# The opening stage written as one sequence: norm, transposes and v's first three products of chunk 0

## The chip, the cores and the metric

The kernel runs on one core of one Trainium2 chip. The metric is the device time of one execution in microseconds (us). Engines are named as in the profile: PE (matrix products; PEld its weight loads), DVE (VectorE), ACT (ScalarE), POOL (GpSimd) and SP (SyncE, which here issues every DMA).

## The reference

`x` has 2048 rows of 1024 values. One layer norm feeds a linear attention with 32 heads and a gated GLU; the two results are multiplied and added to `x`.

```
xn = layernorm(x)                                  # 2048 x 1024
q, k, v = split(xn @ wqkv)                         # 32 heads of 32
phi(a)  = [softmax(a @ w_phi), softmax(-(a @ w_phi))]   # per head, 64 features
o  = phi(q) @ (phi(k)^T v) / (phi(q) @ sum(phi(k)) + 1e-6)
s  = o @ wo
g  = silu((sigmoid(xn @ w_gate) * (xn @ w_up)) @ w_down)    # inner size 3584
out = x + s * g
```

## The kernel before, in words

**Products.** Every large matrix product is cut in two along rows of x, along the inner dimension and along columns, and is done as seven block products in place of eight; their operands are raw blocks (`B11`, `B21`, `B22`) or sums of blocks (`T1` to `T4`). The sums are made once for x and once for the weights. To keep fp32 accuracy each operand is split in two parts, high (a cast by ACT) and low (the difference, by DVE); `split` (L122) issues both, and `mm3` (L127) issues three matmuls of 128x512 (L129, L130, L131) for each pair of parts.

**Order of the work.** The 2048 rows are two chunks of 1024 rows (8 tiles of 128 rows). Chunk 0 comes first: the projections v, k and q, each as seven block products in the order `B11, B21, T2, T3, T4, T1, B22` (48 matmuls each, accumulated in PSUM banks 0 to 3), then the GLU's gate and up products, in which the norm of chunk 1 is done in the background (`x_task`). Chunk 1 follows, then `w_down`, attention and the output.

**The opening.** `x_load` fetches the tiles of x. `norm` (L154) takes statistics on DVE (L161, L162), the root on ACT (L167), the inverse on DVE (L168) and seven tiny steps on POOL (L166, L170 to L175; for chunk 1 on DVE), and normalises a tile on ACT (L177). `transpose` (L187) turns a tile by eight PE transposes (L193) into banks 4 to 7, from where `operand` splits `B11` and `B21`, and ACT copies the raw blocks to SBUF (L197). `x_sums` (L201) forms the sums of blocks: T2 and T3 on DVE, T1 and T4 on POOL (L205). `v_sums` (L248) forms the sums of v's weight blocks, four of two halves each: two on DVE, two on POOL (L253).

**Side steps.** The tiles after the first, `v_sums`, the four K folds, `x_rest` and the four Q folds are a queue (`side`), of which one entry is issued after each quarter of a block product. `fold` (L272) multiplies a raw block of wqk with the per-head `w_phi` on PE (L281, 16 matmuls a fold), copies four results to SBUF on ACT (L282), lets POOL form four sums (`w_sums`, L227 to L230) and stores seven operands to DRAM (`wf_d`, L283), from which the K and Q products later load their weights. K's folds use the SBUF of block `x1` as buffers, two sets by turns, and raw blocks in block `x2`. `x_rest` makes the operands of B22 (in `x1`), T1 (in `x2`) and T4 (in `x6`), so it takes `x1` over once every K fold is stored.

**What sets the order on an engine.** The tile framework's scheduler orders the instructions of each engine by program order and its own time model; each engine then runs its list strictly in order, and waits on semaphores for the others. `tc.issue_after(i)` keeps an instruction behind another one.

Of the kernel before, what the change touches and what calls it, by code (L numbers as in the profile page):

```python
# [2 lines left out]

# [45 lines left out]
def hedgehog_glu_kernel(  # L49
# [17 lines left out]

    ident = sb.tile([P, P], F32, name="ident")
    make_identity(nc, ident)

    wf_d = dram.tile([3, 7, P, 4, HB], F32, name="wf_d")
    wo_d = dram.tile([7, 4, P, 2 * HB], F32, name="wo_d")
# [28 lines left out]
    block("fb", 43, 4, F32)  # L101
    block("fc", 47, 8, F32)
    NW = 8
    WARM = 28

    banks = [psum.tile([P, HB], F32, name=f"bank{i}") for i in range(8)]

    def whole(i):
        return slots[i].rearrange("p a n -> p (a n)")

    def halves(*ids):
        return [slots[i][:, a] for i in ids for a in range(2)]

    def run(i, n):

        name, k = where[i]
        return blocks[name][0][:, k:k + n]
# [4 lines left out]
    def split(o, src):  # L122

        nc.scalar.copy(o[0], src)  # L124
        return nc.vector.tensor_sub(o[1], src, o[0].bitcast(F32))  # L125
# [19 lines left out]
    XO = {B11: 16, T2: 12, T3: 0, B21: 20, T1: 8, T4: 24, B22: 4}  # L145
    tps = Ring(banks[4:])

    last_norm, last_chain = [], []
# [5 lines left out]
    def norm(tiles, xs):  # L154
        n = len(tiles)
        st = small.tile([P, 2, 2, 6], F32, name=f"bn{tiles[0]}", tag="bn")
        mv = small.tile([P, 2, 2], F32, name=f"mv{tiles[0]}", tag="mv")
        ws = small.tile([P, 4, 2], F32, name=f"lnw{tiles[0]}", tag="lnw")
        for i, xt in enumerate(xs):
            for a in range(2):  # L160
                nc.vector.bn_stats(st[:, i, a], xt[:, a * HB:(a + 1) * HB])  # L161
            nc.vector.bn_aggr(mv[:, :, i], st[:, i])  # L162
        v, r, a, b = [ws[:, q, :n] for q in range(4)]
# [6 lines left out]
        eng.tensor_mul(a, r, r)  # L170
        eng.tensor_mul(a, a, v)
        eng.tensor_scalar(b, a, -0.5, 1.5, op0=ALU.mult, op1=ALU.add)
        eng.tensor_mul(r, r, b)
        eng.tensor_mul(b, mv[:, 0, :n], r)
        last_chain[:] = [eng.tensor_scalar(b, b, -1.0, None, op0=ALU.mult).ins]  # L175
        for i, xt in enumerate(xs):
            last_norm[:] = [nc.scalar.activation(xt, xt, AF.Identity, bias=b[:, i:i + 1], scale=r[:, i:i + 1]).ins]  # L177

    def operand(c, i, u, b):

        if c == 0:
            o, cs = run(XO[i], 4), slice(u * P, (u + 1) * P)
            split((o[:, :, 0, cs], o[:, :, 1, cs]), b.rearrange("p (k t) -> p k t", t=P))
        else:
            nc.sync.dma_start(xo_d[i, :, u], b)

    def transpose(t, xt, dst):  # L187

        c, th, u = t // CTT, t % CTT // 4, t % 4
        for q in range(2):  # L190
            tp = tps.next()
            for k in range(4):
                nc.tensor.transpose(tp[:, k * P:(k + 1) * P], xt[:, (4 * q + k) * P:(4 * q + k + 1) * P], ident)  # L193
            i = {(0, 0): B11, (1, 0): B21, (1, 1): B22}.get((q, th))
            if c == 0 and th == 0:
                operand(c, i, u, tp)
            nc.scalar.copy(dst[q], tp)  # L197
            if c and i is not None:
                operand(c, i, u, dst[q])

    def x_sums(c, u, first, second):  # L201
        (b11, b21), (b12, b22) = first, second
        t2 = b22 if c else b12
        for i, o, a, b in ((T1, b11, b12, b11), (T3, b12, b22, b12), (T2, t2, b22, b11), (T4, b21, b21, t2)):
            (nc.vector if c == 0 and i in (T2, T3) else nc.gpsimd).tensor_sub(o, a, b)  # L205
            if c or i in (T2, T3):
                operand(c, i, u, o)

    def load_operand(i):
        o = run(XO[i], 4)  # L210
# [33 lines left out]
    def v_load(i):  # L244
        r, f, kh = ((39, 0, 0), (41, 0, 1), (45, 1, 0), (36, 1, 1))[i]
        nc.sync.dma_start(row4(r), v_block(f, kh))

    def v_sums():  # L248
# [257 lines left out]

    def x_task(t):
        xt = x_load(t, 52)
        norm([t], [xt])
        th, u = t % CTT // 4, t % 4  # L510
        transpose(t, xt, halves(53 + th))
        if th:
            x_sums(t // CTT, u, halves(53), halves(54))

# [167 lines left out]

    XS = (24, 25, 26, 27, 52, 53, 24, 25)
    first = [halves(i) for i in (50, 51, 54, 38)]
    b12s, b22s = Ring(halves(10)), halves(8, 9)
    xts = [x_load(0, XS[0])]  # L690
    phraw = whole(47)[:, :KT * DH].rearrange("p (g f) -> p g f", f=DH)
    nc.sync.dma_start(phraw, w_phi.rearrange("(g p) f -> p g f", p=P))
    v_load(0)
    xts += [x_load(t, XS[t]) for t in range(1, 4)]
    v_load(1)
    xts += [x_load(t, XS[t]) for t in range(4, 6)]

    def x_tiles(*tiles):
        norm(tiles, [xts[t] for t in tiles])
        for t in tiles:  # L700
            if t < 4:
                transpose(t, xts[t], first[t])
            else:
                b = b12s.next(), b22s[t - 4]
                transpose(t, xts[t], b)
                x_sums(0, t - 4, first[t - 4], b)
            if t < 2:
                xts.append(x_load(t + 6, XS[t + 6]))
            if t == 1:
                v_load(2)  # L710
                v_load(3)

    def x_rest():
        for i, name, src in ((B22, "x1", b22s), (T1, "x2", [b[0] for b in first]), (T4, "x6", [b[1] for b in first])):
            block(name, XO[i], 4, F32R)
            for u in range(4):
                operand(0, i, u, src[u])
        fraw.items = halves(43, 54)


    for n in range(WARM):
        nc.tensor.transpose(banks[3][:, n % 4 * P:(n % 4 + 1) * P], ident, ident)
    with tc.high_priority():
        x_tiles(0)
    with tc.issue_after(last_norm[0]):
        while prep():
            pass
    one = whole(44)[:, :P]
    nc.gpsimd.memset(one, 1.0)
    nc.scalar.copy(ones, one)  # L730
    nc.gpsimd.memset(bd, 0.0)

    def phi_blocks():
        with tc.issue_after(last_chain[0]):
            for j in range(4):
                nc.gpsimd.tensor_copy(bd[j * DH:(j + 1) * DH, :, j * DH:(j + 1) * DH], phraw[j * DH:(j + 1) * DH])

    def todo(f, *a):
        side.append(lambda: f(*a))
# [12 lines left out]
    pmm = Ring(banks[:4])  # L752
    gmm = Ring(banks[:4])
    pbank, gbank = {}, {}
    ur = Ring(halves(50, 51))
# [22 lines left out]
                tasks.popleft()()  # L778

    for n, (kind, c, what, i) in enumerate(ops):  # L780
        ws = ready[n]
        if kind == "proj":
            for u in range(4):
                if i in opening:
# [274 lines left out]
```

## Time and profile before

| what | value |
|---|---|
| executions timed, us | 2425.05, 2435.57, 2437.88 (median 2435.57) |
| profiled execution, us | 2428.84, of which the span of instructions is 2427.1 |
| mean granted PE clock | 0.995 |
| PE busy over the span | 2387.5 us (98%) |
| DVE, ACT, POOL busy | 71%, 42%, 41% |
| DMA | 599.44 MB, mean 247 GB/s |

A window line of the profile gives, for a stretch of the span, the busy time of each engine with its number of instructions, the granted PE clock (1.00 is full speed) and the DMA share. A timeline line gives the start, the duration, the engine, the line of the kernel, the operation, what it writes and reads, the count, and in brackets how long the engine was idle before and what released it. Matmuls are pipelined, so a busy PE isn't PE at full rate.

### The profile page before, as it was taken

Reading aid. Unit: us, or ns where it says so; the run is one execution under the profiler, and the core shown is the slowest. Engines: PE = TensorE matmul, PEld = TensorE weight load, DVE = VectorE, ACT = ScalarE, POOL = GpSimd, SP = SyncE. Lnnn points to the kernel's source line nnn. Section 1 sums busy time; section 2 is a strip of 40 time slices with the busy share of each in tenths; the row PEclk is TensorE's granted clock in tenths of the full one; section 3 lists DMA queues with packets and bytes.
Section 4 is the critical chain, followed back from the end, with each engine's and each line's share of the span. In section 5 each row is a group of like instructions: output and inputs, shape, how many; then the busy total and the mean of one; then the engine's idle time right before and its main releaser. Section 6 shows DMA issues by size and latency. Waiting matters only on the chain. (4 is left out here: it accounts for less than half of the span.)

```text
span 2427.1 us, 32021 instructions
## 1 busy us (share of the span) xinstructions
PE 2387.5 (98%) x11076; PEld 1985.6 (82%) x11076; DVE 1717.7 (71%) x2247; ACT 1007.9 (42%) x1499; POOL 991.4 (41%) x665
## 2 busy tenths in 40 slices
PE   7999999999999999999999999999999999999998
PEld 6887888888888878888888888888888887878887
DVE  6546577777777679747867888646888988855555
ACT  6443244445444344324444444423443334443332
POOL 5542245665666432222344232323333435414554
PEclk8999999999999999999999999999999999999999
DMA  7898767777777787787777666686666666877554
GB/s 276 277 342 317 246 234 258 268 262 256 256 266 257 247 292 252 245 284 238 268 265 261 220 218 221 201 294 241 219 239 227 221 210 224 288 237 243 182 175 150
DMA packets 233234, 599.44 MB, mean 247 GB/s; under 512 B 30576, under 2 KB 30576, under 8 KB 228464
## 3 DMA queue, kind: packets, MB, share of 16 engines
q1 hardware_dynamic: 233072, 597.40, 71.4%
q8 instruction: 87, 1.43, 0.2%
q14 instruction: 75, 0.61, 0.1%
HBM read 361.10 MB, written 236.19 MB: 246 GB/s over the span
## 5 line engine op out<-in xcount | busy, mean ns | idle before, releaser
L129 PE MATMUL bank<-x,w 128*128 128x512 f32 x2352 | 912.3, 390 | 4.5 <-DVE fc L914 1.9
L130 PE MATMUL bank<-x,w 128*128 128x512 f32 x2352 | 915.8, 389 | 0.0
L131 PE MATMUL bank<-x,w 128*128 128x512 f32 x2352 | 907.1, 389 | 0.0
L124 ACT CAST w<-fa 128x512 fp32r<-128x512 f32 (+1 forms) x444 | 308.0, 698 | 543.2 <-PE bank L130 377.6
L129 PEld LDWEIGHTS bank<-x,w 128*128 128x128 f32 x2352 | 441.4, 188 | 97.8 <-DVE fc L914 2.3
L125 DVE TENSOR_TENSOR w<-fa,w 128x512 fp32r<-128x512 f32 (+1 forms) x444 | 432.2, 978 | 122.7 <-ACT w L124 113.9
L131 PEld LDWEIGHTS bank<-x,w 128*128 128x128 f32 x2352 | 441.6, 188 | 91.9 <-DVE w L125 0.4
L130 PEld LDWEIGHTS bank<-x,w 128*128 128x128 f32 x2352 | 441.7, 188 | 90.5 <-DVE x L125 0.2
L129 PE MATMUL bank<-w,x 128*128 128x512 f32 x708 | 278.8, 394 | 4.8 <-DVE fb L391 2.3
L131 PE MATMUL bank<-w,x 128*128 128x512 f32 x708 | 278.0, 393 | 1.6 <-DVE x L125 1.6
L130 PE MATMUL bank<-w,x 128*128 128x512 f32 x708 | 277.7, 392 | 0.0
L850 POOL TENSOR_TENSOR fb<-fb,fc 128x512 f32<-128x512 f32 x57 | 88.5, 1552 | 242.8 <-DVE fc L849 217.8
L129 PEld LDWEIGHTS bank<-w,x 128*128 128x128 f32 x708 | 134.0, 189 | 33.6 <-ACT x L124 3.1
L131 PEld LDWEIGHTS bank<-w,x 128*128 128x128 f32 x708 | 133.8, 189 | 29.6 <-DVE x L125 2.3
L590 POOL TENSOR_TENSOR fc<-fc 128x1024 f32<-128x1024 f32 x32 | 81.8, 2556 | 186.2 <-ACT fc L426 131.1
L130 PEld LDWEIGHTS bank<-w,x 128*128 128x128 f32 x708 | 134.0, 189 | 27.2
L125 DVE TENSOR_TENSOR w<-fb,w 128x512 fp32r<-128x512 f32 (+1 forms) x114 | 106.1, 931 | 39.1 <-ACT w L124 37.6
L849 DVE TENSOR_TENSOR fc<-fc,bank 128x512 f32<-128x512 f32 x84 | 57.3, 682 | 101.4 <-PE bank L131 91.9
L124 ACT CAST w<-fb 128x512 fp32r<-128x512 f32 (+1 forms) x114 | 71.4, 626 | 133.6 <-PE bank L130 97.1
L125 DVE TENSOR_TENSOR x<-fa,x 128x512 fp32r<-128x512 f32 x112 | 113.2, 1011 | 19.3 <-ACT x L124 19.0
L602 POOL TENSOR_TENSOR fc<-fc,sa 128x1024 f32<-128x1024 f32 x32 | 70.2, 2193 | 98.3 <-DVE sa L599 98.3
L124 ACT CAST p<-fc 128x512 fp32r<-128x512 f32 x82 | 64.6, 788 | 107.2 <-DVE fc L442 61.0
(254 smaller groups left out, 3266.4 us busy)
## 6 DMA issues: line engine op xcount, KB each, us to landing
ws_d<-w SPq DMA_DIRECT2D x112, 512.0 KB, 3.8
w<-ws_d SPq DMA_DIRECT2D x112, 512.0 KB, 4.8
fa<-w_gu SPq DMA_DIRECT2D x84, 512.0 KB, 3.9
fa<-h_d SPq DMA_DIRECT2D x84, 512.0 KB, 4.2
fa<-wf_d SPq DMA_DIRECT2D x32, 1024.0 KB, 6.7
h_d<-fc SPq DMA_DIRECT2D x120, 256.0 KB, 3.4
fc<-e_d SPq DMA_DIRECT2D x48, 512.0 KB, 3.6
fc<-qkv_d SPq DMA_DIRECT2D x80, 256.0 KB, 4.5
```

Of the source, the lines that this page charges most:

```text
L124: nc.scalar.copy(o[0], src)
L125: return nc.vector.tensor_sub(o[1], src, o[0].bitcast(F32))
L129: nc.tensor.matmul(o, a[0], b[0], start=first, stop=False, **kw)
L130: nc.tensor.matmul(o, a[0], b[1], start=False, stop=False, **kw)
L131: nc.tensor.matmul(o, a[1], b[0], start=False, stop=last, **kw)
L590: nc.gpsimd.tensor_mul(ez, e, zb)
L602: nc.gpsimd.tensor_mul(e3, e3, r2[:, :, None].to_broadcast([P, 32, DH]))
L849: v = nc.vector.tensor_add(b, u2 if q == 3 else u1, bank)
L850: nc.gpsimd.tensor_mul(g, g, b)
```

## The change

Chunk 0's opening is no longer left to the scheduler. A string `FIRST` lists some 170 steps by short names, and `in_order` gives each instruction of PE, DVE, ACT and POOL a dependency on the one before it on its engine, so that each engine keeps the listed order. The steps cover all eight tiles' norm (`bn`, `sq`, `rc`, `ch`, `n`), the transposes (`T`), the splits of x (`xh`, `xl`) and of the weights (`wh`, `wl`), the raw blocks (`k`), the sums T3 and T2 (`T3s`, `T2s`), two weight sums (`s3`, `s2`), the matmuls of v's products B11, B21 and T2 (`m`) and the reading out of B11's and B21's banks (`e`).

Within that: the norm's tiny steps go from seven on POOL to four fused ones on DVE (`scales`, for chunk 1 too); x's first tile and the first weight block are loaded in halves; `w_phi` and the later weight blocks are loaded after all eight tiles; the raw blocks of tiles 0 to 3 are summed on POOL from the two split parts, where ACT copied them from PSUM; T2 of x is T3 plus B11; the low part of B21's weights is made on POOL; T2's weights need two sums (both on DVE), and two further sums follow on POOL; five more warming transposes stand ahead of the first tile. After `FIRST`, POOL is kept to the order `phi_blocks`, `t4`, `v_sums`, `t1`. All that is left of the side queue (the folds, `x_rest`, the stores of two weight sums) is issued after the last listed instruction of every engine. All of v's B11, B21 and T2 now end before the first fold.

The core of the diff:

```diff
-        eng = nc.gpsimd if tiles[0] < CTT else nc.vector
-        eng.tensor_scalar_add(v, mv[:, 1, :n], EPS_LN)
-        nc.scalar.activation(a, v, AF.Sqrt)
-        nc.vector.reciprocal(r, a)
-        eng.tensor_mul(a, r, r)
...
+        fused = nc.vector.scalar_tensor_tensor
+        def rest():
+            fused(a, v, EPS_LN, r, op0=ALU.add, op1=ALU.mult)
+            fused(a, a, -0.5, r, op0=ALU.mult, op1=ALU.mult)
+            fused(r, a, 1.5, r, op0=ALU.add, op1=ALU.mult)
+            fused(b, mv[:, 0, :n], -1.0, r, op0=ALU.mult, op1=ALU.mult)
...
-    v_first = {B11: 39, B21: 41, T2: 39, T3: 45, T4: 39, T1: 36, B22: 41}
+    v_first = {B11: 39, B21: 41, T2: 36, T3: 45, T4: 45, T1: 39, B22: 41}
...
     def v_sums():
-        vec, pool = nc.vector.tensor_tensor, nc.gpsimd.tensor_tensor
-        for f, o, a, b, op in ((vec, 3, 2, 3, "add"), (vec, 2, 0, 2, "subtract"),
-                               (pool, 0, 3, 0, "subtract"), (pool, 1, 1, 0, "subtract")):
+        for o, a, b, op in ((0, 3, 0, ALU.add), (1, 1, 3, ALU.subtract)):
             for h in range(2):
-                f(whole(VA[o] + h), whole(VA[a] + h), whole(VA[b] + h), op=getattr(ALU, op))
-        for i in (T2, T3, T1, B22):
+                v_sum(nc.gpsimd, o, a, b, op, h)
...
+        elif kind == "k":
+            t, q = int(rest[0]), int(rest[1])
+            if t < 4:
+                hi, lo = [o.bitcast(F32) for o in operand((B11, B21)[q], t)]
+                nc.gpsimd.tensor_add(by_k(first[t][q]), hi, lo)
+            else:
+                nc.scalar.copy((b12s, b22s)[q][t - 4], xbank(t, q))
...
+                nc.vector.tensor_sub(t3s[u], b22s[u], b12s[u])
+                nc.vector.tensor_add(t2s[u], t3s[u], first[u][0])
...
+    with in_order(mybir.EngineType.PE, mybir.EngineType.DVE, mybir.EngineType.Activation, POOL):
+        for name in FIRST:
+            (do_other if name[0] in "mewT" or name.startswith("n0q") else do)(name)
...
+    with after_first():
+        for u in range(4):
+            split(operand(T3, u), by_k(t3s[u]))
+        v_store(T2, T3)
+        while prep():
+            pass
+    with in_order(POOL):
+        phi_blocks()
+        t4()
+        v_sums()
+        t1()
...
-    todo(x_tiles, 1)
-    todo(lambda: (x_tiles(2, 3), phi_blocks()))
-    todo(x_tiles, 4, 5)
-    todo(v_sums)
-    todo(x_tiles, 6, 7)
     for k in range(4):
         todo(fold, K, k)
     todo(x_rest)
+    todo(v_store, T1, B22)
     for k in range(4):
         todo(fold, Q, k)
```

More of the change, by code (lines that the diff above doesn't have):

```diff
@@ L179, in operand @@
[L179 to L199, printed above, removed]
@@ L201, in x_sums, with scales, root, inverse @@
-    def x_sums(c, u, first, second):
-        (b11, b21), (b12, b22) = first, second
[L203 to L207, printed above, removed]
+    def scales(n, mv, ws):
+        v = mv[:, 1, :n]
+        r, a, b = [ws[:, q, :n] for q in range(3)]
+        fused = nc.vector.scalar_tensor_tensor
+        def root():
+            nc.scalar.activation(a, v, AF.Sqrt, bias=eps)
+        def inverse():
+            nc.vector.reciprocal(r, a)
+        def rest():
[3 more added lines that the diff above has]
+            fused(b, mv[:, 0, :n], -1.0, r, op0=ALU.mult, op1=ALU.mult)
+        return root, inverse, rest
@@ new lines, in stats, with norm @@
+    def stats(t, n=1):
+        st = small.tile([P, 2, 2, 6], F32, name=f"bn{t}", tag="bn")
+        mv = small.tile([P, 2, 2], F32, name=f"mv{t}", tag="mv")
+        ws = small.tile([P, 3, 2], F32, name=f"lnw{t}", tag="lnw")
+        return st, mv, ws
+    def norm(t, xt):
+        st, mv, ws = stats(t)
+        for a in range(2):
+            nc.vector.bn_stats(st[:, 0, a], xt[:, a * HB:(a + 1) * HB])
+        nc.vector.bn_aggr(mv[:, :, 0], st[:, 0])
+        for f in scales(1, mv, ws):
+            f()
+        nc.scalar.activation(xt, xt, AF.Identity, bias=ws[:, 2, :1], scale=ws[:, 0, :1])
@@ new lines, in operand, with by_k, transposed, x_sums @@
+    def operand(i, u):
+        o, cs = run(XO[i], 4), slice(u * P, (u + 1) * P)
+        return o[:, :, 0, cs], o[:, :, 1, cs]
+    def by_k(b):
+        return b.rearrange("p (k t) -> p k t", t=P)
+    def transposed(t, q, xt, tp):
+        for k in range(4):
+            nc.tensor.transpose(tp[:, k * P:(k + 1) * P], xt[:, (4 * q + k) * P:(4 * q + k + 1) * P], ident)
+    def x_sums(u, first, second):
+        (b11, b21), (b12, b22) = first, second
+        for i, o, a, b in ((T1, b11, b12, b11), (T3, b12, b22, b12), (T2, b22, b22, b11), (T4, b21, b21, b22)):
+            nc.gpsimd.tensor_sub(o, a, b)
+            nc.sync.dma_start(xo_d[i, :, u], o)
@@ L508, in x_task @@
         xt = x_load(t, 52)
-        norm([t], [xt])
+        norm(t, xt)
         th, u = t % CTT // 4, t % 4
-        transpose(t, xt, halves(53 + th))
+        for q in range(2):
+            tp, b = tps.next(), slots[53 + th][:, q]
+            transposed(t, q, xt, tp)
+            nc.scalar.copy(b, tp)
+            i = {(0, 0): B11, (1, 0): B21, (1, 1): B22}.get((q, th))
+            if i is not None:
+                nc.sync.dma_start(xo_d[i, :, u], b)
         if th:
-            x_sums(t // CTT, u, halves(53), halves(54))
+            x_sums(u, halves(53), halves(54))
     dsteps = [(i, j, (0, 1)) for i in order[:-1] for j in range(NJ)]
@@ L683, in attend @@
         return out
-    XS = (24, 25, 26, 27, 52, 53, 24, 25)
+    XS = (24, 25, 26, 27, 52, 53, 6, 7)
     first = [halves(i) for i in (50, 51, 54, 38)]
-    b12s, b22s = Ring(halves(10)), halves(8, 9)
-    xts = [x_load(0, XS[0])]
-    phraw = whole(47)[:, :KT * DH].rearrange("p (g f) -> p g f", f=DH)
-    nc.sync.dma_start(phraw, w_phi.rearrange("(g p) f -> p g f", p=P))
[L693 to L711, printed above, removed]
+    b12s, b22s = halves(10, 26), halves(8, 9)
+    t3s, t2s = halves(52, 53), halves(27, 24)
+    xts = [whole(i) for i in XS]
+    for a in range(2):
+        nc.sync.dma_start(slots[XS[0]][:, a], x[:P, a * HB:(a + 1) * HB])
+    for h in range(2):
+        nc.sync.dma_start(slots[39 + h], v_block(0, 0)[:, 2 * h:2 * h + 2])
+    for t in range(1, 4):
+        x_load(t, XS[t])
+    v_load(1)
+    for t in range(4, 8):
+        x_load(t, XS[t])
+    v_load(2)
+    v_load(3)
+    phraw = slots[11][:, 1, :KT * DH].rearrange("p (g f) -> p g f", f=DH)
+    nc.sync.dma_start(phraw, w_phi.rearrange("(g p) f -> p g f", p=P))
     def x_rest():
@@ L716, in x_rest @@
             for u in range(4):
-                operand(0, i, u, src[u])
+                split(operand(i, u), by_k(src[u]))
         fraw.items = halves(43, 54)
[L721 to L727, printed above, removed]
     one = whole(44)[:, :P]
@@ new lines, in normalized, with xbank, x_parts, w_parts @@
+    def normalized(t, cs=slice(0, D)):
+        _, _, ws, i, _ = scale[t]
+        nc.scalar.activation(xts[t][:, cs], xts[t][:, cs], AF.Identity, bias=ws[:, 2, i:i + 1], scale=ws[:, 0, i:i + 1])
+    def xbank(t, q):
+        return banks[4 + (2 * t + q) % 4]
+    def x_parts(t, q):
+        if q == "t":
+            return operand(T2, t - 4), by_k(t2s[t - 4])
+        return operand((B11, B21)[q], t), by_k(xbank(t, q))
+    def w_parts(n, h):
+        o = run(28 + (4 * n + 2 * h) % NW, 2)
+        return (o[:, :, 0], o[:, :, 1]), slots[v_first[order[n]] + h]
@@ new lines, in hedgehog_glu_kernel, with in_order @@
+    for n in range(WARM):
+        nc.tensor.transpose(banks[3][:, n % 4 * P:(n % 4 + 1) * P], ident, ident)
+    queued = {}
+    @contextmanager
+    def in_order(*engines):
+        traced = nc.cur_bb.bb.instructions
+        last = traced[-1]
+        yield
+        start = next(k for k in reversed(range(len(traced))) if traced[k] is last) + 1
+        for i in traced[start:]:
+            if i.engine in engines:
+                if i.engine in queued:
+                    tc.add_manual_dep(i, queued[i.engine].name,
+                                      mybir.DependencyInfo(mybir.DependencyClass.NoSync, mybir.DependencyReason.DATA),
+                                      reason="in_order")
+                queued[i.engine] = i
@@ L746, in hedgehog_glu_kernel, with entry @@
+    with in_order(POOL):
[3 more added lines that the diff above has]
+        t1()
+    def todo(f, *a):
+        def entry():
+            with after_first():
+                f(*a)
+        side.append(entry)
     for k in range(4):
@@ L783, in hedgehog_glu_kernel @@
             for u in range(4):
+                if n == 2:
+                    pbank[u] = pmm.next()
+                    step()
+                    continue
                 if i in opening:
```

137 lines of the change are left out of this document (112 added, 25 removed).

## The prediction

> **What bounds the kernel now.** I began with the busy time by stretch, to see where PE, busy 98% of the span, still loses time.
>
> ```profile
> core 0: us, PE busy (x) PEld busy (x) DVE busy (x) ACT busy (x) POOL busy (x), PEclk, DMA share, GB/s
> 0.00:60.00 60.00, 46.10 (x212) 38.79 (x213) 38.08 (x57) 40.56 (x62) 32.20 (x55) 0.83 0.75 276
> 60.00:120.00 60.00, 57.93 (x339) 49.49 (x338) 34.98 (x40) 26.02 (x43) 33.10 (x23) 1.00 0.83 276
> 120.00:200.00 80.00, 77.60 (x368) 64.60 (x367) 39.53 (x42) 29.38 (x43) 32.73 (x23) 1.00 0.94 330
> 200.00:800.00 600.00, 600.00 (x2681) 497.48 (x2680) 424.20 (x574) 263.24 (x387) 320.70 (x220) 1.00 0.74 261
> ```
>
> At full clock a 128x512 matmul follows the last one after 0.2275 us and a 128x128 after 0.0905 us (timeline, 200 us and later). The timeline has 98 and 114 of them before 60 us: 22.3 + 10.3 = 32.6 us of work, so 27.4 us are lost there. From 60 to 200 us it has 470 and 234, 128.1 us of work: 11.9 us lost. From 200 to 800 us nothing is lost. So only the first 200 us, 39.3 us of loss in all, can be won by this change. PE's waits up to 120 us say on what:
>
> ```profile
> engine line waited for: us in total, times, longest us
> PE bank L193 <- ACT x L177: 5.7, 2, 3.3
> PE bank L193 <- ACT x L197: 3.6, 1, 3.6
> PE bank L131 <- DVE x L125: 1.6, 1, 1.6
> ```
>
> They are the norm's chain and the raw copies, which the change attacks; the rest of the loss is half clock (PEclk 0.83). But POOL and DVE hinder each other, and the change moves work between these two, so I looked at their timelines next (DVE, then POOL, then ACT).
>
> ```profile
> 58.92 1.75 DVE L125 TENSOR_TENSOR x<-fc,x 128x512 fp32r<-128x512 f32 x1
> 60.60 1.78 DVE L125 TENSOR_TENSOR x<-x,x 128x512 fp32r<-128x512 f32 x1
> 62.30 0.68 DVE L125 TENSOR_TENSOR x<-fc,x 128x512 fp32r<-128x512 f32 x1
> ```
>
> ```profile
> 68.36 1.74 POOL L227 TENSOR_TENSOR x<-x 128x512 f32<-128x512 f32 x1
> ...
> 96.60 1.29 POOL L230 TENSOR_TENSOR x<-x 128x512 f32<-128x512 f32 x1
> ```
>
> ```profile
> 107.08 2.18 ACT L124 CAST x<-x 128x512 fp32r<-128x512 f32 x4 [6.53 <-DMA qkv_d<-fc]
> 109.16 0.58 ACT L282 COPY fc<-bank 128x512 f32<-128x512 f32 x1
> 110.26 1.66 ACT L124 CAST x<-fc 128x512 fp32r<-128x512 f32 x3 [0.52 <-DVE x L125]
> ```
>
> A DVE step with both inputs in SBUF takes 0.68 us alone and 1.75 beside a POOL sum; that sum takes 1.27 to 1.30 alone and 1.62 to 1.85 beside such steps: they go by turns, about 1.7 us a pair. The four K folds' 16 sums run from 68.36 to 97.89 us. 9.2 us later, their stores landed, ACT splits B22's operand (107.08) over the folds' buffers and, behind it, T1's (110.26); PE begins v's product T1 at 114.3, just as it is done with T4. So this second chain is nearly critical already.
>
> **How I worked it out.** I followed the changed program's lists, engine by engine, giving each instruction its row's duration and starting it when its engine, its semaphores and the DVE/POOL turn allow; loads land 2.35 us and stores 1.4 us after issue, plus 0.66 us for each 256 KB (before's landings). The same on the old lists loses 27.9 us up to 60 (trace 27.4), ends the K sums at 98.2 (97.89) and loses 32.2 up to 200 (39.3, so it misses 7). All "by the lists" below is this.
>
> **The front.** The first tile lands in halves, some 3.8 and 4.4 us (512 KB landed at 4.57). POOL's seven steps ran from 6.21 to 8.56, 2.35 us; four fused DVE steps at the 0.19 us pitch of chunk 1's one-input steps take 0.8. Normalising half a tile takes 0.62 for 1.24 (L177). The first matmul comes at 9.4 for 12.26. Then 64 transposes and 144 matmuls, 38.6 us of work, must pass. By the lists the waits left are tile 1's norm 2.1 us, tile 2's 3.8, later tiles' 2.5, T2's operands 1.2, and half clock from 22 to 29. T2 ends at 62; 17.6 us are lost up to 60 for 27.4. **Gain: 10 us.** Raw copies leave ACT (8 of 0.57 us); their eight POOL sums of 1.28 and B21's low part (2 of 2.40) lie in POOL's idle time, at the price of hindering the chains: tile 2's four fused steps run 18.1 to 22.5 for 0.8 us.
>
> What those steps cost beside POOL is bounded by chunk 1's norm, already on DVE:
>
> ```profile
> L173 DVE TENSOR_TENSOR lnw<-lnw 128x1 f32<-128x1 f32 x8 | 8.4, 1049 | 0.3
> L170 DVE TENSOR_TENSOR lnw<-lnw 128x1 f32<-128x1 f32 x8 | 6.4, 802 | 0.3
> L174 DVE TENSOR_TENSOR lnw<-mv,lnw 128x1 f32<-128x1 f32 x8 | 1.3, 159 | 0.3
> ```
>
> Each is 0.16 us when POOL rests and about 1.05 on average when it works. The Trainium skill (SBUF — State Buffer, "Who interferes with whom") says that whichever of the two starts second blocks for the other's whole instruction; by that alone, an estimate, four fused steps could each wait out a 2.40 us weight split, 9.6 us for tile 2's chain where I put 4.4, and the front's gain would be 5 us less.
>
> **T3.** Its weights' low parts stand on DVE behind the four splits of T3's x, which take turns with `t4` on POOL (1.7 us each): PE waits 5.6 us, 61 to 67. It is a new wait, and the clock falls to half for a while after it.
>
> **POOL's chain, the costly part.** After `FIRST` POOL must do `t4`, `v_sums`, `t1`, then the folds' sums. `t4` begins with T2's last block, which DVE delivers at 54: its steps up to there are 38 us back to back (from 4 us on: 42), the rest is waiting. Then 4 x 1.7 for `t4`, 4 x about 2.9 for `v_sums` (rows: 2.40 alone) and 4 x 1.28 for `t1`: 6.8 + 11.6 + 5.1 = 23.5, to 78. Before, `v_sums` lay at 28.6 to 39.2 under PE's matmuls and the K sums began at 68.36. The 16 sums at 1.7 take 27 us and have three gaps, 6.6 us together: fold 2 reuses fold 0's buffers, whose stores stand on SP behind the store of T4's first bank, which waits for DVE (87 to 93). They end at 112 for 97.9. Stores (8.7 us, beside two 1 MB loads) and the splits of B22 and then T1 (3.7 us) follow as before: **T1 begins at 124.5 for 114.3.** PE has done T4 at about 99 and has only fold blocks (0.72 us each) until then.
>
> So the front's 10 us are given back in this stall: whatever ends T2 earlier ends in the same wait.
>
> **The sum.** T1 begins 10.2 us later, with 23 fold blocks behind it for 23.9: +0.7. After the stall PE runs at half clock: the row of before is 6.8 us of it after the idle time at 47 to 51 (granted clock 0.67 from 50 to 60 us), +3.4; the shortest is none. By the Trainium skill (TensorE: Matmul & The Clock Gate, "What's actually happening") one busy window of 3.4 us brings it back, an estimate of +1.7. I take +2.5, between none and the row's worst. Of the 4.3 us that before loses after T1's start, 1.8 are waits for fold loads, which now fall into the stall: -1.8. Together **+11.6**. In chunk 1's norm the tiny DVE steps go from seven to four, but all four read two SBUF tiles: saved 3 x 0.15 us, or up to 1.05 more; by the lists ACT's normalise and the sigmoid behind it come 1.3 us late for PE at four of the eight tiles, 5 us at most, and before loses nothing there. I take +1.5. The warming transposes (5 x 0.09 to 0.18), the later `w_phi` and the stores cost nothing: PE waits for tile 0 anyhow, and `w_phi` lands at about 25 for a need at 38. If the cover were gone they would cost under 1 us. **In all +13 us.**
>
> Against its own time the sum gives 2428.84 + 13 = 2441.8. That execution lies 6.7 under the median of 2435.57, inside the timed 2425.05 to 2437.88; the four shown average 2431.8, and I forecast from there: **2445 us.** 0.5%, about what a measurement here can tell from no change, is 12 us.
>
> **Rivals.**
> - *POOL's chain is in time (not slower).* If T2's last block came at 42, or the 28 POOL steps took their lone durations (8 x 1.28 + 4 x 2.40 + 16 x 1.28 = 40 us, from 54 to 94), and SP had nothing in front, T1 could begin near 106 and most of the front's 10 us would stay: -6, 2426 us. Each us by which the K sums end before 112 gives one back, and level is at about 100. For it: POOL idles 14 us before 54. Against: DVE is 38 us full there, and before, with less on POOL, the sums already went by turns.
> - *Chunk 1's norm stalls PE too.* All four late sigmoids and worse half clock: +20 to +24, 2454 us. For it: L173's 1.05 us; against: before loses nothing with the same collisions.
> - *The sequence slips.* If the front kept none of its gain, T1's start would move little, since POOL's chain starts from DVE, not from PE: +13 to +18. That the order isn't kept is out: the lists show it.
>
> **Chances.** The forecast (T1 waits for POOL's chain, +6 to +20) 0.62; POOL in time 0.20; chunk 1 too 0.13; others 0.05. Over +12 lie 0.62 of the forecast's 0.62 and all of chunk 1's: 0.52. Faster than -12 needs POOL in time and a gain that the front's 10 us don't hold alone: 0.07. Within 0.5%: 0.41. The range leaves about one in ten out at either end: 2427, where POOL in time begins, to 2458, the forecast's worst with chunk 1's 5 us.
>
> **What would show it.** First matmul near 9.4 us; T2 done near 62; K sums from 78 to 112 on POOL beside DVE steps of 1.7 us; T1's first matmul near 124, after some 20 us of little PE work with the clock at half; up to four gaps of 1.3 us between 430 and 800. It is wrong if PE is never idle between 95 and 125, if the K sums end before 100, or if the front keeps less than 5 us.

## The result and the profile after

The changed kernel takes 2455.85 us (median of 2454.8, 2456.85, 2454.84, 2457.57) beside 2436.62 for the kernel before on the same chip: ratio 1.009, 95% interval 1.0064 to 1.0117. It is slower, by about 22 us by that ratio (the medians lie 19 apart). The profiled execution took 2454.8 us with a span of 2453.0 us, for 2428.84 and 2427.1 before.

First the busy time by stretch of the changed kernel, with the columns of the prediction's view and the stretches that matter now:

```profile
core 0: us, PE busy (x) PEld busy (x) DVE busy (x) ACT busy (x) POOL busy (x), PEclk, DMA share, GB/s
0.00:60.00 60.00, 51.64 (x254) 42.73 (x255) 51.87 (x83) 38.53 (x58) 25.95 (x27) 0.97 0.58 213
60.00:120.00 60.00, 44.51 (x253) 38.88 (x251) 28.32 (x23) 18.84 (x30) 40.82 (x25) 0.86 0.90 315
120.00:200.00 80.00, 75.91 (x360) 63.57 (x360) 29.62 (x37) 30.23 (x47) 28.15 (x20) 0.94 0.85 282
200.00:300.00 100.00, 94.21 (x404) 77.47 (x403) 55.05 (x66) 32.87 (x45) 17.27 (x12) 0.97 0.80 286
```

Counting each matmul at its full-clock step, as the prediction does, the time that PE loses is:

| stretch, us | before | after |
|---|---|---|
| 0 to 60 | 27.4 | 17.3 |
| 60 to 100 | 5.2 | 9.6 |
| 100 to 150 | 4.2 | 23.0 |
| 150 to 200 | 2.5 | 1.7 |
| 200 to 300 | -0.3 | 8.6 |
| 300 to 800 | -0.4 | 2.2 |

The first 60 us won 10 us; 60 to 150 us gave back 23. Up to 200 us that makes 12.3 us more than before, where 11.6 had been forecast. Then 200 to 300 us costs another 8.9 and 300 to 800 another 2.6: 23.8 of the 25.9 us by which the two spans differ.

PE's waits from 60 to 300 us name the places:

```profile
engine line waited for: us in total, times, longest us
PE bank L285 <- DMA fc<-wqkT: 11.1, 2, 5.7
PE bank L131 <- DVE fb L395: 5.8, 1, 5.8
PE bank L132 <- DVE w L127: 4.6, 1, 4.6
```

The third row is T3's wait (62 to 67 us). The first is T1's stall: PE has nothing but fold blocks (L285), and these wait for their loads. The second was in no sum: the end of K's product T3, at 203.6 us. It isn't wholly new. In the kernel before PE already waited at that place, at 188 us:

```profile
PE bank L129 <- DVE fb L391: 2.3, 1, 2.3
```

T1's stall on POOL and then on ACT (timeline):

```profile
78.51 1.34 POOL L227 TENSOR_TENSOR x<-x 128x512 f32<-128x512 f32 x1 [0.91 <-ACT w L126]
...
89.04 1.91 POOL L227 TENSOR_TENSOR x<-x 128x512 f32<-128x512 f32 x1 [3.87 <-DMA wf_d<-x]
...
98.15 1.27 POOL L227 TENSOR_TENSOR x<-x 128x512 f32<-128x512 f32 x1 [3.12 <-DMA wf_d<-x]
...
110.78 1.26 POOL L227 TENSOR_TENSOR x<-x 128x512 f32<-128x512 f32 x1 [6.41 <-DMA wf_d<-x]
...
114.80 1.27 POOL L230 TENSOR_TENSOR x<-x 128x512 f32<-128x512 f32 x1
```

```profile
123.28 2.18 ACT L126 CAST x<-x 128x512 fp32r<-128x512 f32 x4 [6.75 <-DMA wf_d<-x]
126.46 1.66 ACT L126 CAST x<-fc 128x512 fp32r<-128x512 f32 x3 [1.00 <-DVE x L127]
```

Four folds of four sums each: every fold after the first starts with a wait for a store of an earlier fold (`wf_d<-x`), 13.4 us in all. When the last fold is stored, ACT splits B22's operand over the fold buffers (123.28) and then T1's (126.46); PE begins T1 at 127.1. B22's split begins 0.2 us after the last store out of the fold buffers has landed (123.1 us in the trace). Between 80 and 120 us the 16 DMA engines have no pause (a share of 1.04 and 369 GB/s, for 0.88 and 291 before).

The wait at K's T3, on the timelines of SP, POOL and DVE:

```profile
190.09 0.32 SPq L392 DMA_DIRECT2D qkv_d<-fc  x1
190.46 1.32 SPq L266 DMA_DIRECT2D fb<-wo  x2
```

```profile
206.72 1.59 POOL L230 TENSOR_TENSOR fb<-fb 128x512 f32<-128x512 f32 x1
```

```profile
205.89 1.30 DVE L127 TENSOR_TENSOR fc<-fb,fc 128x512 fp32r<-128x512 f32 x1 [3.30 <-ACT fc L126]
207.11 1.75 DVE L127 TENSOR_TENSOR p<-fb,p 128x512 fp32r<-128x512 f32 x1
208.97 0.69 DVE L395 TENSOR_TENSOR fb<-fc,bank 128x512 f32<-128x512 f32 x1
```

`o_sums` makes wo's block sums in the background of the products, in four parts: loads (L266), splits (L126, L127), four POOL sums (L227 to L230), stores (L272). Its second part works in slots 45 and 46 (`fb`), and the evacuation of K's T3 (L395) writes to the same slots. The loads are issued at 190.5 us, behind a store of K's B21 on SP; the evacuation can begin only at 208.97, and PE stands from 204.0 to 209.8. In the kernel before, those loads went out 18 us earlier, and the evacuation began at 190.1:

```profile
172.37 0.78 SPq L262 DMA_DIRECT2D fb<-wo  x1
```

### The profile page after: what moved, and what is told of

Its sections match the earlier page's. It is cut to its first block, busy times and chain, and to the rows that moved or that the text cites. A ratio compares the mean times of both kernels' runs of the same rounds, so it can differ in the third digit from the quotient of the medians.

```text
span 2453.0 us, 31998 instructions
## 1 busy us (share of the span) xinstructions
PE 2397.1 (98%) x11081; PEld 1993.2 (81%) x11081; DVE 1718.9 (70%) x2241; ACT 1005.6 (41%) x1492; POOL 988.9 (40%) x641
## 4 chain that ended last, share of the span: by engine, by line
PE 82%; DVE 8%; DMA 5%; issue 2%; ACT 2%; POOL 1%; SPq 0%; ACTq 0%; DVEq 0%; POOLq 0%
PE bank L131 27%; PE bank L132 26%; PE bank L133 26%; DVE w L127 1%; PE bank L465 1%; DVE x L127 1%; DMA wf_d<-x 1%; DMA fc<-xo_d 1%; PE bank L643 1%; DVE p L127 1%; DMA fc<-qkv_d 1%; PE bank L285 0%; ACT w L126 0%; DMA fa<-wf_d 0%; DMA fb<-w_down 0%
## 5 line engine op out<-in xcount | busy, mean ns | idle before, releaser
L126 ACT CAST w<-fa 128x512 fp32r<-128x512 f32 (+1 forms) x438 | 301.7, 693 | 556.2 <-PE bank L132 384.4
L127 DVE TENSOR_TENSOR w<-fa,w 128x512 fp32r<-128x512 f32 (+1 forms) x438 | 424.1, 972 | 125.7 <-ACT w L126 118.5
L600 POOL TENSOR_TENSOR fc<-fc 128x1024 f32<-128x1024 f32 x32 | 82.1, 2566 | 183.5 <-ACT fc L430 128.4
L127 DVE TENSOR_TENSOR w<-fb,w 128x512 fp32r<-128x512 f32 (+1 forms) x116 | 108.1, 933 | 39.2 <-ACT w L126 34.3
L126 ACT CAST w<-fb 128x512 fp32r<-128x512 f32 (+1 forms) x116 | 73.3, 633 | 138.1 <-PE bank L132 102.1
L127 DVE TENSOR_TENSOR x<-fa,x 128x512 fp32r<-128x512 f32 x112 | 114.7, 1024 | 17.6 <-ACT x L126 17.2
L126 ACT CAST p<-fc 128x512 fp32r<-128x512 f32 x82 | 64.6, 788 | 110.5 <-DVE fc L446 61.7
```

The costliest lines, as they stand in the source:

```text
L600: nc.gpsimd.tensor_mul(ez, e, zb)
```

## The experiments

Losses are PE's, counted as above; line numbers are each kernel's own. Ratios are to the kernel before, run beside; the changed kernel's is 1.009.

**1. `v_sums` ahead of `t4` on POOL.**

```
         phi_blocks()
-        t4()
         v_sums()
+        t4()
         t1()
```

> POOL's list after the planned sequence is phi, v_sums, t4, t1 instead of phi, t4, v_sums, t1; all else as changed. In the changed kernel t4 heads that list and starts at 54 us, because DVE delivers T2's last block only then, and POOL stands before it. Theory A (the stall before T1 is POOL's chain, and what sets its start is the sharing with DVE, not the wait at its head): v_sums now run beside DVE's last steps of the planned sequence and hinder them, the operands of T2 and T3 come later, T3's first matmul at 70 or later instead of 67, T1's at 127 to 130 (changed: 127.1); total +0 to +6 us on the changed kernel. Rival B (POOL merely stands idle behind t4's wait): v_sums fill that idle time, the K sums begin 8 to 12 us earlier than 78.5, T1 at 116 to 120, total -6 to -11 us.

Measured: 2460.79 us, ratio 1.0124 (1.0109 to 1.0139). T3 begins at 72.8 us for 62.1, its wait for the weights' low parts is down to 0.9 (4.6), T1 begins at 133.4. `v_sums` did fill POOL's idle time, but DVE's steps to T2 came late, the loss up to 60 us rose to 26.0, and T1 came 6 us later, beyond theory A's 130; the total is some 8 us over the changed kernel's by the ratios, beyond its 6 too. Rival B is out: filling POOL's idle time in this way brings T1 no earlier.

**2. K's fold sums on DVE.**

```
-        nc.gpsimd.tensor_add(a22, a21, a22)   # and the three subtractions
+        eng.tensor_add(a22, a21, a22)         # eng = nc.vector for K's folds
```

> The K folds' sixteen sums go on DVE instead of POOL (0.68 us each alone, 11 us in all, instead of 1.27 to 1.75). Theory A (POOL's chain of t4, v_sums, t1 and the K sums holds back v's product T1): the sums no longer queue behind t1, the last K sum comes by about 108 instead of 116, T1 begins at 119 to 123 instead of 127.1, total -3 to -6 us. Rival B (the fold buffers and their stores, which stand in SP's queue behind the store of T4's first bank, set the pace, whoever adds): last K sum and T1 within 2 us of the changed kernel's, total within 2 us. Rival C (DVE is then late with evacuations and weight splits): T1 no earlier, new PE waits for DVE before it, total slower by 3 or more.

Measured: 2449.39 us, ratio 1.0086 (1.0066 to 1.0106), not to be told from the changed kernel. On the timelines of this kernel, DVE's first sum of the second to fourth fold, and then ACT's split of B22:

```profile
91.91 0.69 DVE L227 TENSOR_TENSOR x<-x 128x512 f32<-128x512 f32 x1 [1.92 <-DMA wf_d<-x]
...
102.39 0.69 DVE L227 TENSOR_TENSOR x<-x 128x512 f32<-128x512 f32 x1 [2.81 <-DMA wf_d<-x]
...
108.95 0.69 DVE L227 TENSOR_TENSOR x<-x 128x512 f32<-128x512 f32 x1 [1.07 <-DMA wf_d<-x]
```

```profile
124.34 2.18 ACT L126 CAST x<-x 128x512 fp32r<-128x512 f32 x4 [4.86 <-DMA fc<-wqkT]
```

The sums end 4 us earlier (111.8 us) and T1 still begins at 128.4. That is rival B for T1 and the total, though its sums were to end within 2 us. Twelve us pass between the last sum and the split: the last store out of the fold buffers is issued only at 115.5, behind two weight loads on SP, and lands at 124.2, and the split begins 0.15 us later (the view names a load that landed at the same moment). This took away the simple reading that T1 waits for whoever does the additions.

**3. wo's second sum one operation earlier.** `n in (7, 9, 11, 13)` becomes `n in (7, 8, 11, 13)`.

> The second of wo's four background sums is launched behind K's product T2 (operation 8 of the order) instead of behind K's T3 (operation 9); all else as changed. In the changed kernel PE stands 5.9 us at 203.6, at the end of K's product T3, because that product's evacuation goes to the buffers that this background sum still uses. Theory A (the second half of the missed time is this one collision, the sum lying about 3 us later to PE than before the change): the wait of 5.9 us with its half clock is gone or under 2.5 us, the loss of 8.6 us between 200 and 300 us falls to under 3, total -5 to -8 us on the changed kernel (about 2449). Rival B (the lateness of SP's, ACT's and POOL's queues after T1's stall costs PE the same wherever that sum is put): a wait of about the same length turns up at another product, total within 2 us. The stall before T1 is untouched in both: T1 at 127.

Measured: 2453.16 us, ratio 1.0092 (1.0077 to 1.0107). The wait stays, 4.9 us at 203.6: theory A missed. The loads went out at 190.3, as before the edit. The kernel itself keeps each of these sums behind the last store issued (`tc.issue_after(last_load[0])`), and that is B21's last one in both places: in the kernel's list operation 8 is K's B21 and 9 its T2, not T2 and T3 as the expectation has it. This edit didn't free the buffer earlier, so it left open whether the buffer was the cause; experiment 7 asks that.

**4. Chunk 1's norm in its old seven steps.** `x_task`'s four fused steps go back to `tensor_scalar_add`, `tensor_mul` and the rest.

> Chunk 1's norm (eight tiles, run in the background of chunk 0) goes back to seven DVE steps after the square root instead of four fused ones; chunk 0's planned sequence keeps its fused steps. Theory A (PE's four waits of 0.7 us for the sigmoid's input between 454 and 806 us come from the fused steps, which all read two tiles of SBUF beside POOL): the four waits go, loss from 400 to 800 us back to 0.0 from 2.3, total -2 to -3 us, that is not to be told from the changed kernel by times alone. Rival B (they come from the lateness of that background work, whatever its form): the four waits stay at 0.5 to 1.3 us each, total within 1 us.

Measured: 2454.0 us, ratio 1.0094 (1.0079 to 1.0109). In the changed kernel PE waited four times, 0.6 us each, for a sigmoid (`ACT fb L1014`: 2.5 us in all); these waits are gone, and the loss from 400 to 800 us goes from 2.3 to -0.2. Theory A, and as expected the time alone doesn't show it.

**5. and 6. K's folds without their sums; K's folds without their stores.**

```
-        w_sums(lambda i, b: nc.sync.dma_start(wf_d[which, i, :, k], b), *bs)
+        # 5: for K the four additions are left out
+        # 6: for K the seven stores are left out; K's weight loads read a block of wv
```

> Leaves out the K folds' sixteen sums (K's folded weights are then the raw blocks); all loads, PE blocks, copies and stores of the folds stay. Putting the sums on DVE made the kernel some 4 us faster but did not bring T1 forward (128.4 for 127.1 us), so two theories stand. Theory A (POOL's work sets the K folds' pace): with nothing left to add, folds end 12 us or more earlier, T1 begins at 110 to 114, the loss between 100 and 150 us falls from 23 to under 12. Theory D (transfers set it: the 16 DMA engines are busy 102 to 107 % from 80 to 120 us, since the folds' loads and stores, v's stores and T4's and T1's weight loads all come after 70 us, where before the change they began at 52): the folds still pass at the rate of their 44 transfers, T1 at 120 or later, loss in 100 to 150 us above 17.

> Leaves out the 28 stores of the K folds' results (7 MB) and lets K's products read a block of wv in their place, by loads of the same size; all sums stay on POOL. Theory A (POOL's work sets the pace): the sums still begin at 78.5 us and take turns with DVE, last K sum no earlier than 108, T1 at 114 or later. Theory D (transfers, and the reuse of the fold buffers behind the stores, set it): the three gaps of 13.4 us among the K sums go, DMA's share from 80 to 120 us falls below 0.8, last K sum by 103, T1 at 105 to 110, loss between 100 and 150 us under 10 for 23.

Measured: 2446.47 us (ratio 1.0053, 1.0032 to 1.0073) and 2446.61 (1.0053, 1.0033 to 1.0073). T1 begins at 116.2 without the sums (loss from 100 to 150 us 15.2) and at 109.5 without the stores (5.7), for 127.1 (23.0). Without sums neither theory's numbers are met: it lies between. Without stores theory D's are, but for the last sum, which ends at 104.8 for 103: no waits for a store are left among the sums, and DMA's share from 80 to 120 us is 0.73. So a fold's round is a chain (load, PE, copy, sums, store, and the buffers free for the next fold but one), and both parts lengthen it, the stores more. The second barrier moved the other way:

```profile
PE bank L131 <- DVE fb L396: 12.3, 1, 12.3
```

That is PE's wait at K's T3 in the kernel without stores, for 5.8. K's T4 behind it begins at 197.5 us for 209.8, so of the 17.6 us by which T1 came forward 12.3 are left there.

**7. wo's second sum in another buffer.**

```
-    o_sums(k, halves(*((52, 53), (45, 46))[k % 2])) for k in range(4)
+    o_sums(k, halves(*((52, 53), (45, 46))[k == 3])) for k in range(4)
```

> The second of wo's four background sums works in the buffer of the first (52, 53) instead of the one (45, 46) that K's product T3 evacuates to; its launch is that of the changed kernel. Launching it one operation earlier had left the wait at 203.6 us in place (5.0 us), because its four loads stand in SP's queue behind a store of K's product B21 at 190 us in either case. Theory A (that wait is this buffer still being read by the background sum): the wait is gone or under 1 us with nothing like it within 15 us, loss between 200 and 300 us below 2 for 8.6, total -6 to -9 us. Rival B (DVE and ACT are late there for other reasons): a wait of 3 us or more stays between 195 and 225 us, total within 2 us. T1's stall is the same in both.

Measured: 2450.16 us, ratio 1.0071 (1.0055 to 1.0088). The wait at 203.6 is gone, one of 1.7 us is left at 221; the loss from 200 to 300 us is 2.4 for 8.6, the profiled execution 6.75 us shorter (2448.05). T1 begins at 128.0. This is theory A for the wait, so the buffer is its cause. The total gains about 5 us by the ratios, less than the 6 expected at least, and its interval overlaps that of the changed kernel.

**8. K's folds 2 and 3 in buffers of their own, and the splits of B22, T1 and T4 ahead of them.**

```
-    fblock = {K: Ring(((4, 5), (6, 7))), Q: Ring(((50, 51), (52, 53)))}
+    fblock = {K: Ring(((4, 5), (6, 7), (52, 53), (50, 51))), Q: Ring(((52, 53), (50, 51)))}
...
-    for k in range(4):
+    for k in range(2):
         todo(fold, K, k)
     todo(x_rest)
+    for k in range(2, 4):
+        todo(fold, K, k)
```

> K's folds 2 and 3 work in the buffers (52, 53) and (50, 51) instead of returning to (4, 5) and (6, 7), which become B22's operand, and the splits of B22, T1 and T4 stand in the lists ahead of these two folds instead of behind them. Theory A (T1 waits for B22's buffer, that is for four folds in a row): T1 begins at 103 to 109 us for 127.1, when two folds are stored, the loss between 100 and 150 us falls from 23 to under 8; but K's product T3 then still meets wo's second background sum in its buffers (45, 46), by the lists for up to 17 us near 185, so the total gains only 3 to 12 us. Rival C (PE gets through v's products but then waits as long for K's first weights, which need all four folds): a wait of over 8 us before K's first product at 125 to 135 us, total within 3 us.

Measured: 2452.33 us, ratio 1.0079 (1.0064 to 1.0094). T1 begins at 104.0, the loss from 100 to 150 us is 8.9: the stall is gone. And PE's waits from 60 to 300 us begin thus:

```profile
PE bank L131 <- DVE fb L395: 20.3, 1, 20.3
PE bank L132 <- DVE w L127: 4.7, 1, 4.7
```

T1 came forward by 23 us, and K's T4 begins at 209.7 us, where it began before (209.8). Theory A for T1, with a little more loss than the 8 us expected; the total's gain is under the 3 us expected at least, because the second barrier took nearly all of it. The edit changes the buffers and the order of the lists together, so it does not part the two.

Why K's T4 begins at the very moment of the changed kernel is not shown. The loads of wo's second part go out at 174.9 us here, 15.6 us earlier than there, yet its last POOL sum ends at 210.1: in between, ACT's splits of these slots wait for stores of wo's own earlier results.

```profile
201.77 0.62 ACT L126 CAST fc<-fb 128x512 fp32r<-128x512 f32 x1 [4.31 <-DMA wo_d<-fc]
205.89 0.62 ACT L126 CAST fc<-fb 128x512 fp32r<-128x512 f32 x1 [2.55 <-DMA wo_d<-fc]
```

**9. Both edits (7 and 8).**

> Both edits together: K's folds 2 and 3 in buffers of their own with the splits of B22, T1 and T4 ahead of them, and wo's second background sum in buffer (52, 53). Alone the first took T1's stall away (loss from 100 to 150 us 8.9 for 23.0) and the wait at K's product T3 grew from 5.9 to 20.4 us, ending at 209.7 us, just where it ended before; the second alone took that wait away and left T1's stall (24.4). Theory A (two barriers in a row, each of which alone holds PE to about the same time, so that the gains add only when both go): no wait over 3 us from 70 to 300 us, loss from 0 to 300 us at 36 to 44 for 60, total -17 to -23 us on the changed kernel (2434 to 2440; ratio to the kernel before about 1.000 to 1.003). Rival B (a third barrier stands right behind, Q's folds or wo's sums): a new wait of over 8 us between 130 and 300 us, total -5 to -10.

Measured: 2432.07 us for 2431.28 of the kernel before, ratio 0.9999 (0.999 to 1.0008). No wait from 60 to 300 us but T3's is over 2 us (PE's waits):

```profile
PE bank L132 <- DVE w L127: 4.7, 1, 4.7
PE bank L285 <- ACT fc L286: 1.8, 3, 0.7
PE bank L285 <- DMA fc<-wqkT: 1.7, 2, 1.4
```

The busy time by stretch, in the columns of the first view above:

```profile
0.00:60.00 60.00, 51.23 (x251) 41.80 (x251) 51.35 (x82) 38.12 (x57) 25.42 (x27) 0.94 0.58 213
60.00:120.00 60.00, 53.58 (x290) 45.36 (x289) 37.46 (x36) 19.95 (x32) 31.73 (x17) 0.94 0.79 269
120.00:200.00 80.00, 76.86 (x392) 64.65 (x391) 32.19 (x35) 32.13 (x48) 39.75 (x28) 1.00 0.97 329
200.00:300.00 100.00, 99.17 (x438) 81.81 (x437) 57.99 (x71) 35.41 (x51) 25.85 (x18) 1.00 0.87 321
```

The opening is that of the changed kernel; the clock stays full from 120 us on, and PE is busy 9 us more from 60 to 120 and 5 us more from 200 to 300 us. The loss up to 300 us is 38.1, for 60.1 of the changed kernel and 39.0 of the kernel before. Theory A. Together the two edits win about 22 us by the ratios (0.9999 for 1.009), which is the whole of what the change cost. Alone, experiment 8 won about 3 and experiment 7 about 5, neither clear of the noise.

**10. The same with the old chunk-1 norm and wo's four sums launched one operation later** (`n in (8, 10, 12, 14)`).

> Like the kernel with both edits, and chunk 1's norm in its seven old steps, and each of wo's four background sums launched one operation later (8, 10, 12, 14 for 7, 9, 11, 13). Theory A (PE's four waits of 0.7 us between 440 and 810 us come from the fused steps): they go, -2 to -3 us on the kernel with both edits; and the later launch leaves SP's queue free for K's stores: any wait of 1 to 2 us near 220 us goes too. In all 2430 to 2437, ratio to the kernel before 0.997 to 1.001. Rival: the later launch pushes wo's sums into the first units of what follows, a new wait of 2 us or more between 250 and 320 us, total no better than the kernel with both edits.

Measured: 2427.86 us, ratio 0.9984 (0.9974 to 0.9993): faster than the kernel before by some 4 us, and by as much ahead of experiment 9. The loss from 300 to 800 us is down to -0.2 (3.0 in experiment 9). The time is below the 2430 to 2437 us expected, the ratio within its range. The two edits in it were not run apart on this kernel.

**11. The kernel before with the edits 7 and 8.**

> The kernel before, with the same two edits of the buffers (K's folds 2 and 3 apart, splits of B22, T1 and T4 ahead of them; wo's second sum in (52, 53)). Theory A (only the changed kernel's front ran into these two buffers): the kernel before has nothing there to lose (loss from 100 to 300 us 6.4), so it stays within 4 us of itself; its first 60 us keep their loss of 27. The changed kernel with both edits is then level with it or ahead by up to 5 us, because the front's 10 us come through only less the wait before T3 (4.9). Rival B (the edits help any front): total -5 us or more on the kernel before.

Measured: 2426.68 us, ratio 0.9978 (0.9968 to 0.9988). It wins 5 us, a little more than theory A allowed (the rival's figure), and is level with experiment 10, whose interval overlaps. Up to 60 us experiment 10 loses 17.5 us where this kernel loses 27.5; from 60 to 150 us it loses 17.5 where this one loses 8.7. Like for like, with the edits 7 and 8 alone, the changed kernel (experiment 9) is some 5 us slower than this one, and their intervals do not overlap. So even with both barriers out of the way the planned opening gains nothing that these runs can tell; what holds PE from 60 to 150 us then was not taken apart beyond T3's wait (experiment 12).

**12. Experiment 10 with T3's weights split ahead of T3's second x block.**

```
-        for u in range(4):
-            split(operand(T3, u), by_k(t3s[u]))
-        v_store(T2, T3)
+        split(operand(T3, 0), by_k(t3s[0]))
         while prep():
             pass
+        for u in range(1, 4):
+            split(operand(T3, u), by_k(t3s[u]))
+        v_store(T2, T3)
```

> Like the kernel with both edits, the old chunk-1 norm and the later launches, with T3's weights split ahead of the second to fourth blocks of T3's x (in the changed kernel PE waits 4.9 us from 62 to 67 us for these weights' low parts on DVE, behind four splits that take turns with t4 on POOL). Theory A (that wait is only the order of the list): it falls under 2 us, total -2 to -4 us on the kernel without this edit. Rival B (DVE's whole work up to T4 is what PE waits for, so the wait moves to the start of T4): the wait before T3 shrinks, one of 2 us or more turns up between 78 and 86 us, total within 1.5 us.

Measured: 2428.61 us, ratio 0.9991 (0.9982 to 1.0). The wait before T3 is gone, one of 1.7 us stands before T4 at 81 us, and the fold blocks' waits around 100 us are longer; T1 begins at 103.7 in both. Rival B, with a slightly smaller wait than it named.

## Why the prediction was right or wrong

**Right: the front.** First matmul 9.7 us (forecast 9.4), T2 done at 62.05 (62), front gain 10.1 (10). Tile 2's four fused steps run from 18.83 to 23.23, the 4.4 us that was put down. The Trainium skill's rule (SBUF — State Buffer, "Who interferes with whom") would have let each of the four wait for a whole POOL step; here they took 0.63, 2.31, 1.19 and 0.16 us. The trace agrees with the rule in kind, for the first three ended at 19.46, 21.81 and 23.04 us, each just as the POOL step beside it ended (19.45, 21.80, 23.02). But only one met a whole split of 2.4 us, so the bound of 9.6 us was not near.

**Right: T3's new wait,** 4.6 to 4.9 us for 5.6.

**Near in size, half right in cause: T1's stall.** T1 began at 127.1 for 124.5, and the loss up to 200 us grew by 12.3 for 11.6. That closeness is partly luck: the loss before 200 us in the kernel before includes its wait of 2.3 us at K's T3, which in the changed kernel lies behind 200 us. Without it the growth is nearly 15 us. The K sums ran from 78.5 to 116.1 for 78 to 112: the three gaps took 13.4 us for 6.6, the sums themselves about 24 for 27. The prediction blamed POOL's sums taking turns with DVE, and said that each us by which they end earlier gives one back. In experiment 2 they ended 4.3 us earlier on DVE, and T1 began 1.3 us later. Experiments 5, 6 and 8 show a chain of four folds through two sets of buffers, and the split ahead of T1 began some 0.2 us after the last store out of these buffers had landed in the changed kernel and in experiments 2, 5 and 8 (123.1, 124.2, 112.1 and 99.1 us). That full DMA engines make these stores late is not shown: the last one took 6.8 us from issue to landing, for 7.2 in the kernel before. A reading of the windows would fit it, though no run tested it by itself: up to 60 us the changed kernel moved 213 GB/s for 276, 3.8 MB less, which at the 369 GB/s of the stretch from 80 to 120 us is 10 us of transfers. By this reading PE's front ran ahead of its data by as much as it had gained. The rival "POOL's chain is in time" would have needed more than lone POOL steps: with no K sums at all T1 still came at 116.2, not 106.

**The half clock.** Taken as +2.5 us after T1. Matmuls step at 0.427 us instead of 0.2275 for 3.3 us after T1's start, 5.2 after T3's wait and 5.9 after the one at K's T3, which costs about half of each: 1.6, 2.6 and 2.9 us. In the stall itself the granted clock was 0.50 from 109.9 us on, so the fold blocks in it ran at half rate too. The Trainium skill (TensorE: Matmul & The Clock Gate, "What's actually happening") asks for at least one busy window of about 3.4 us and says that the window runs freely; the trace agrees, with about one to nearly two such windows.

**Right: chunk 1's norm,** four waits, at 2.5 us for 1.5, and experiment 4 shows that the fused steps cause them. The rival that named this norm gave 2454 us, near the measured time, but not for its reason: the norm is 2.5 us of it.

**Wrong: the sum ends too early.** The failed step is the sum behind T1's start. It charged "23 fold blocks behind it for 23.9: +0.7", took 1.8 us off for fold loads, and let the rest of before's loss behind T1 stand unchanged; after 200 us it put nothing but the norm, since "nothing is lost" there before. That loss behind T1 was put at 4.3 us; counted from 114.25 to 200 us it is 5.3, of which the wait at K's T3 is 2.3. This wait was the first place that anything late would come up against. In the changed kernel K's B21 is stored later, wo's loads go out right behind its last store, and wo's second part comes 18 us later (190.5 for 172.4) while PE is 15 us later at that product. The wait grew from 2.3 to 5.8 us and brought nearly 3 us of half clock: some 6 us that no term held (less than the 8.9 us of the stretch from 200 to 300 us, because in the kernel before the wait lay ahead of 200 us). With the 3 us by which T1's part came out larger, and 1 us more for the norm, that is about the distance from 13 us to the measured 22. Experiment 7 shows the buffer to be the cause of the wait. Experiment 8 shows that it acts as a barrier: PE was held there to the same moment although T1 came 23 us earlier. What sets that moment stays open; where the folds had fewer sums or stores (experiments 5 and 6) K's T4 began 8 and 12 us earlier, less than T1 had gained.

**The base.** The forecast stood on 2431.8 for the kernel before. Beside the experiments the kernel before had medians of 2429.36, 2433.73 and 2431.28, so the base was fair; the size was 13 us where about 22 were measured.

## What to carry to other kernels

A stall that is "given back" must be followed past its end: list every later place where the old trace already shows PE waiting for a buffer, even 2 us, and carry the lateness of each background task to it. Two buffer reuses in a row act like two gates: opening one moved the time by 3 to 5 us, which the noise may hide, opening both by 22. And when compute is brought forward, compare the bytes moved up to the same point, not only the engines' busy time: here the changed kernel was behind by some 10 us of transfers, as much as its front had gained, though no run tested that this is what it lost.

## What the runs showed of the hardware

Moving sixteen sums from POOL to DVE left T1's start where it was (128.4 us for 127.1), while leaving out K's stores brought it to 109.5. The 16 DMA engines had no pause from 80 to 120 us in the changed kernel (share 1.04, 369 GB/s) and some without K's stores (0.73, 246 GB/s).

After waits of 4.6, 5.8 and 20.3 us (changed kernel twice, experiment 8) PE ran at half clock for 5.2, 5.9 and 3.7 us, so the length did not follow that of the wait. The half clock had set in while PE still waited: in experiment 8 the granted clock was 0.50 from 192.9 us, 3.5 us into the wait, to 213.4. Waits of 1.7 us (experiment 7, at 221 us) and 2.3 us (kernel before, at 188) left the granted clock at 1.00.
